# One TensorE loop body for both layers of a two-layer decode step

## The chip, the cores and the metric

One core of one Trainium2 chip runs the kernel as a single program. The metric is the device time of that program in microseconds. The core has five engines with instruction streams of their own: TensorE (PE in the profile; its weight loads are listed apart as PEld), VectorE (DVE), ScalarE (ACT), GpSimd (POOL) and SyncE (SP). Sixteen DMA engines move data between the device memory and the on-chip SBUF; TensorE adds up its products in eight PSUM banks of 128 partitions by 512 floats.

## The reference

The reference is one decode step of two equal layers. Each is a grouped-query attention over a cache of 32768 positions, followed by a gated feed-forward; both layers use the same caches and weights.

```
def layer(x):                                   # x: 2 x 1 x 512
    q = layernorm(x) @ wq                       # 2 x 32 heads x 128
    s = einsum("bhqd,bhkd->bhqk", q, k) * 128 ** -0.5   # 8 KV heads, 4 query heads on each
    o = einsum("bhqk,bhkd->bhqd", softmax(s), v)
    x = x + o.reshape(2, 1, 4096) @ wo
    g, u = layernorm(x) @ w_gate, layernorm(x) @ w_up   # 512 x 1792 each
    return x + (gelu(g) * u) @ w_down
out = layer(layer(x))
```

All is float32. The caches hold 2 x 8 x 32768 x 128 numbers each, and every layer needs all of both.

## The kernel before, in words

**Data.** SBUF has one pool, `mem`, of 110 units of 128 x 512 floats (256 KB each). The work of a layer is 16 pairs of a KV head and a batch row. A pair has 64 units of K and 64 of V, read in halves of 32 units, 8 MB each, and a half is 64 KB on each partition. The list `stream` holds all transfers in the order in which SP issues them; `plan` gives each its place in `mem`, and `pump` issues the next one as soon as its place is free. A place comes free when TensorE has multiplied with what lies there: SP waits for TensorE's semaphore and then issues. Layer 1 takes the pairs in the opposite order, so that K and V of the last pair of layer 0 serve the first pair of layer 1 without a second read. Because room is short there, six units are parked in the PSUM banks `S`, `T`, `M` during the change of layers (`stash`) and come back in the first pair's scores (line 728).

**A pair on TensorE.** `scores` (line 716) issues 64 products of 32 x 512, 32 into each bank of `S`. `softmax` follows on DVE and ACT with two small TensorE steps (lines 746, 759). `values` (line 782) issues 64 groups of two products of 16 x 512 into bank `A`, 128 in all, and `combine` (line 801) transposes four pieces. In layer 0 these go into `A`; in layer 1 they go into a bank of `M`. Line 811 (`project`) multiplies the first seven heads with `wo` in the last turn of a layer.

**The order of the work.** A recording layer (`Program`) notes every operation, derives the semaphore waits, and writes each engine's stream. ACT, DVE, POOL and SP get theirs straight. TensorE's is written by `run_tensor`: straight code (part 0), a loop over the 16 turns of layer 0, straight code (part 1), a loop over the 16 turns of layer 1, straight code (part 2). A loop body is values of turn n-1, then scores and softmax of turn n. Turn 0 of each layer (its scores and softmax) stands in the straight code ahead of the loop. A wait whose value differs from turn to turn reads a register, set before the loop and raised in each turn. What happens in one turn alone stands in the body under a branch (`apart`, `alone`, `more`).

**Between the layers.** After the last pair come the last head's product, `residual`, the gate and up products, `gelu`, the down product in pieces (`WD_SPLIT`), `residual` again, and the queries of layer 1, all fed by transfers of 0.25 to 2 MB. `warm` issues products that nobody reads.

**Banks there.** Layer 1's queries go into `A`, and so do layer 0's second `residual` and the first half of the scores of layer 1's turn 0:

```
        banks = [A, S[1]] if second else S
```

because `S[0]` holds a parked unit at that time.

Of the kernel before, what the change touches and what calls it, by code (L numbers as in the profile page):

```python
# [42 lines left out]
ROLLED = range(1, LAST + 1)  # L43
# [15 lines left out]
WO_PARTS = [[(0, 28), (28, 4)], [(4, 28), (0, 4)]]  # L59
# [62 lines left out]
class Program:  # L122
# [157 lines left out]
    def rolled(self, layer):  # L280


        by_place, apart, alone, more, waits = {}, {}, {}, {}, {}
        for op in self.ops:
            if op.turn and op.turn[0] == layer:
                if op.apart:
                    apart.setdefault(op.place, {}).setdefault(op.turn[1], []).append(op)
                else:
                    by_place.setdefault(op.place, []).append(op)
        order = sorted({*apart, *by_place}, key=lambda x: (SECTIONS.index(x[0]), x[1]))  # L290
        for place, ops in by_place.items():
            turns = [op.turn[1] for op in ops]
            assert turns == list(range(ROLLED[0], LAST + (place[0] == "values")))
            assert len({(o.where, str(o.extents), o.by) for o in ops}) == 1, "turns differ"
            waits[place] = here = []
            for key in {k for o in ops for k in o.waits}:
                v = [o.waits.get(key) for o in ops]
                known = [i for i, x in enumerate(v) if x is not None]
                if known == [len(ops) - 1] and turns[-1] == LAST:
                    low = max([x.value for x in self.ops[:ops[0].order] if x.key == key and x.by] or [0])  # L300
                    assert 0 < low < v[-1]
                    more.setdefault(turns[-2], []).append((place, key, v[-1] - low))
                    here.append((key, low, 0))
                    continue
                if len(known) < 3:
                    for i in known:
                        alone.setdefault(place, {}).setdefault(turns[i], []).append((key, v[i]))
                    continue
                steps = [(v[j] - v[i]) // (j - i) for i, j in zip(known, known[1:])]
                step = max(set(steps), key=steps.count)  # L310
                for i, o in enumerate(ops):
                    if v[i] is None:
                        near = min(known, key=lambda j: abs(i - j))
                        so_far = max([x.value for x in self.ops[:o.order] if x.key == key and x.by] or [0])
                        v[i] = min(max(v[near] + step * (i - near), 1), so_far)
                    assert v[i] > 0
                if v[1] < v[0] + step:
                    alone.setdefault(place, {}).setdefault(turns[0], []).append((key, v[0]))
                    v[0] = v[1] - step
                for i, (x, y) in enumerate(zip(v, v[1:])):  # L320
                    if y != x + step:
                        more.setdefault(turns[i], []).append((place, key, y - x - step))
                here.append((key, v[0], step))
        return order, by_place, waits, alone, more, apart

    def emit(self):
# [21 lines left out]
        def loop(e, layer):  # L348
            order, by_place, waits, alone, more, apart = self.rolled(layer)
            regs = {}  # L350
            for place, here in waits.items():
                for key, first, _ in here:
                    regs[place, key] = e.alloc_register(f"w{layer}_{len(regs)}")
                    e.reg_mov(regs[place, key], first)

            def places(section, n):
                for place in order:
                    if place[0] != section:
                        continue
                    for t in sorted({*alone.get(place, ()), *apart.get(place, ())}):  # L360
                        with e.If(n == t):
                            straight(e, apart.get(place, {}).get(t, ()))
                            for key, value in alone.get(place, {}).get(t, ()):
                                e.wait_ge(self.sems[key], value)
                    if place in by_place:
                        one(e, by_place[place][0], [(key, regs[place, key]) for key, _, _ in waits[place]])

            with e.Fori(ROLLED[0], LAST + 1) as n:
                places("values", n)
                with e.If(n != LAST):  # L370
                    places("project", n)
                    places("scores", n)
                    for t, here in sorted(more.items()):
                        with e.If(n == t):
                            for place, key, x in here:
                                e.reg_add(regs[place, key], regs[place, key], x)
                    for place, here in waits.items():
                        for key, _, step in here:
                            if step:
                                e.reg_add(regs[place, key], regs[place, key], step)  # L380

        def run_tensor(e):
# [39 lines left out]
SECTIONS = ["values", "project", "scores"]  # L422
# [11 lines left out]
def block_kernel(nc, x, kt, vt, wq, wo, gu, wd, out):  # L434
# [80 lines left out]
    def rolled(kind, l, n):  # L515
        return n in ROLLED if kind == "k" else True

    def add_wo(l, i):
        s, m = WO_PARTS[l][i]
        add(("wo", l, i), wo[:, s * DM:(s + m) * DM], m * DM)  # L520
# [94 lines left out]

    def heads(g):
# [53 lines left out]
    def queries(l):  # L670
        qp = small(A)
        for j, (s, m) in enumerate(pieces(WQ_SPLIT[l])):
            w = get(("wq", l, j), m)
            for i in range(s, s + m):
                (k, v), t = divmod(i // 4, 2), i % 4
                pe.matmul(qp[32 * t:32 * t + 32, :], window(k, v), w[:, i - s, :],  # L676
# [12 lines left out]
        for v in range(2):  # L689
            dve.tensor_copy(qin[:, :, v], src[:, :, :, NB * v:NB * v + NB].rearrange("p h t b -> p t b h"))  # L690
        return qt

    def stage(l, n):
        if n < len(ORDER):
            g, b = ORDERS[l][n]
            dve.tensor_copy(qpad, qall[:, REP * (NB * g + b):REP * (NB * g + b) + REP])

    def scores(l, n, g, b):
        first, second = meets(l, n)
        mx = tiny("mx")  # L700
        banks = [A, S[1]] if second else S
# [6 lines left out]
        for key, o, s, m in todo:  # L708
            if key is None:
                w = mem[:, o * UNIT:(o + m) * UNIT].rearrange("p (a c) -> p a c", a=m)  # L710
            else:
                w = get(key, at[key][0][1] if key in at else m)[:, o:o + m, :]
            for j in range(s, s + m):
                u, c, t = j // 32, j // QUAD % 8, j % QUAD
                tile_of = [i for i in order if i // 32 == u and i % QUAD == t]
                pe.matmul(banks[u][32 * t:32 * t + 32, :], pad[:, PAD_Q - 4 * c:PAD_Q + 32 - 4 * c],  # L716
                          w[:, j - s, :], start=(j == tile_of[0]), stop=(j == tile_of[-1]))
                if j == [i for i in order if i // 32 == u][-1]:
                    dve.tensor_reduce(mx[:, u:u + 1], banks[u], axis=AX.X, op=OP.max)  # L719
# [6 lines left out]
            elif second and key[1] == 0 and A_AT + o == BACK:  # L726
                for bank, i, copy in zip(where, range(WAIT), 3 * [act.copy, dve.tensor_copy]):
# [4 lines left out]
        return mx, banks  # L732
# [9 lines left out]
    def softmax(mx, banks):  # L742
# [9 lines left out]
        for u in range(2):  # L752
            act.activation(T[u], banks[u], AF.Exp, bias=bias, scale=SCALE, accum_out=ls[:, u:u + 1])  # L753
# [13 lines left out]
    def values(l, n, g, b, p):  # L767
# [23 lines left out]
    def combine(l, n, linv, g, b):  # L791
        if n == LAST - 1:
            act.activation(desk[:, :256], A[:, :256], AF.Copy, scale=linv)
            dve.tensor_scalar(desk[:, 256:], A[:, 256:], linv, None, op0=OP.mult)
            with pr.apart_of():
                warm(128, W[:NB], False)
        else:
            act.activation(desk, A, AF.Copy, scale=linv)  # L798
        m = small() if l else A
# [3 lines left out]
        dve.tensor_reduce(heads(g)[:, :, b], diag, axis=AX.XY, op=OP.add)  # L803

    def project(l):
        s, m = WO_PARTS[l][0]
        w = get(("wo", l, 0), m)
        turns = [g for g, _ in ORDERS[l][1::2]][:-1]
        for g in turns:
            for t in range(REP):  # L810
                pe.matmul(W[32 * t:32 * t + NB, :], heads(g)[:, t, :], w[:, REP * g + t - s, :],  # L811
                          start=(g == turns[0]), stop=(g == turns[-1]))
# [18 lines left out]
    def last_head(l, g):  # L831
        s, m = WO_PARTS[l][1]
        w = get(("wo", l, 1), m)
        for t in range(REP):
            add_row(heads(g)[:, t, :], w[:, t, :], t == REP - 1)
        done(("wo", l, 1))

    def residual():
# [5 lines left out]
        warm(128)  # L844
        m = small(A)[:, :2 * KC * NB].rearrange("p (i c b) -> p i c b", i=2, b=NB)
# [9 lines left out]
    def feedforward(l):  # L855
# [35 lines left out]
        tops = sum(WD_SPLIT[l][:1 if l else 2])  # L891
# [27 lines left out]
        for j, m in enumerate(WD_SPLIT[l]):  # L919
# [3 lines left out]
            elif not l and 1 <= j <= 2:  # L923
                if j == 1:
                    warm(256)
                    hidden(1)
                else:
                    warm(512)
# [14 lines left out]
    for l in range(2):  # L943
# [4 lines left out]
        for n in range(LAST + 1):  # L948
            with pr.turn_of(l, n) if n in ROLLED else nullcontext():
# [5 lines left out]
                if n == LAST - 1:  # L955
                    pr.section("project")
                    with pr.apart_of():
                        project(l)
                        turn(xin, side())
                pr.section("scores")  # L960
# [5 lines left out]
                found = softmax(*found)  # L966
# [4 lines left out]
        last_head(l, g)  # L971
        residual()
# [54 lines left out]
```

## Time and profile before

| what | value |
|---|---|
| median of 3 runs | 2557.25 us (2557.09 to 2557.37) |
| the profiled execution: its own time | 2557.27 us |
| its span, first to last instruction | 2555.8 us |
| TensorE busy, products | 1228.2 us, 48% of the span |
| read from device memory | 1102.58 MB, 431 GB/s over the span |
| mean granted TensorE clock | 0.748 |

The span leaves 1.47 us of the execution's time outside it. A busy share is a mean over the whole span; the rows below say which wait ends last in each stretch. Clock shares are of 2.4 GHz.

### The profile page before, as it was taken

Reading aid. Unit: us, or ns where it says so; the run is one execution under the profiler, and the core shown is the slowest. Engines: PE = TensorE matmul, PEld = TensorE weight load, DVE = VectorE, ACT = ScalarE, POOL = GpSimd, SP = SyncE. Lnnn points to the kernel's source line nnn. Section 1 sums busy time; section 2 is a strip of 40 time slices with the busy share of each in tenths; the row PEclk is TensorE's granted clock in tenths of the full one; section 3 lists DMA queues with packets and bytes.
Section 4 is the critical chain, followed back from the end, with each engine's and each line's share of the span. In section 5 each row is a group of like instructions: output and inputs, shape, how many; then the busy total and the mean of one; then the engine's idle time right before and its main releaser. Section 6 shows DMA issues by size and latency. Waiting matters only on the chain.

```text
span 2555.8 us, 19801 instructions
## 1 busy us (share of the span) xinstructions
PE 1228.2 (48%) x9177; PEld 320.9 (13%) x9177; DVE 145.8 (6%) x495; ACT 81.4 (3%) x189; POOL 2.7 (0%) x9
## 2 busy tenths in 40 slices
PE   3444445354455354354684553544544544534456
PEld 1011111011011011111121110111111111101112
DVE  0000000000000000000010000000000000000001
ACT  0000000000000000000000000000000000000000
POOL 0000000000000000000000000000000000000000
PEclk8677777777777777776897767777777777767788
DMA  9999999999999999999999999999999999999999
GB/s 426 428 439 431 435 432 431 438 432 437 431 431 436 432 437 431 435 432 431 427 418 436 434 433 436 433 433 434 431 437 432 435 433 432 435 433 434 434 433 386
DMA packets 25091, 1102.91 MB, mean 432 GB/s; under 512 B 2792, under 2 KB 2928, under 8 KB 5616
## 3 DMA queue, kind: packets, MB, share of 16 engines
q1 hardware_dynamic: 25056, 1102.65, 99.9%
q8 instruction: 12, 0.20, 0.0%
q14 instruction: 7, 0.06, 0.0%
q10 hardware_dynamic: 16, 0.00, 0.0%
HBM read 1102.58 MB, written 0.07 MB: 431 GB/s over the span
## 4 chain that ended last, share of the span: by engine, by line
DMA 74%; PE 23%; SPq 1%; another core or an unknown queue 0%; DVE 0%; issue 0%; ACT 0%
DMA mem<-in_kt 37%; DMA mem<-in_vt 35%; PE S L716 12%; PE A L782 11%; DMA mem<-in_wd 1%; SPq L487 1%; DMA mem<-in_wq 1%; DMA mem<-in_gu 1%; PE A L676 0%; PE W L829 0%; PE A L716 0%; ACT T L753 0%; DVE desk L755 0%; DVE aux L719 0%
## 5 line engine op out<-in xcount | busy, mean ns | idle before, releaser
L716 PE MATMUL S<-mem,aux 128*32 128x512 f32 x4032 | 512.1, 666 | 617.3 <-DMA mem<-in_kt 617.3
L782 PE MATMUL A<-mem 128*16 128x512 f32 x2048 | 292.3, 732 | 477.6 <-DMA mem<-in_vt 477.6
L782 PE MATMUL A<-mem,desk 128*16 128x512 f32 x2048 | 286.2, 722 | 32.4 <-DMA mem<-in_vt 17.7
L716 PEld LDWEIGHTS S<-mem,aux 128*32 128x32 f32 x4032 | 133.7, 121 | 972.6 <-DMA mem<-in_kt 639.7
L782 PEld LDWEIGHTS A<-mem 128*16 128x16 f32 x2048 | 62.2, 113 | 705.5 <-DMA mem<-in_vt 507.6
L719 DVE TENSOR_REDUCE aux<-S 128x1 f32<-128x512 f32 x63 | 43.5, 691 | 1130.7 <-PE S L716 1130.7
L782 PEld LDWEIGHTS A<-mem,desk 128*16 128x16 f32 x2048 | 64.6, 111 | 227.4 <-issue 209.4
L753 ACT ACTIVATE T<-S,aux 128x512 f32<-128x512 f32 x63 | 41.4, 657 | 1196.7 <-DVE aux L749 1196.7
L759 PE MATMUL M<-aux 128*128 128x4 f32 x64 | 14.5, 298 | 85.2 <-DVE aux L757 85.2
L798 ACT ACTIVATE desk<-A,aux 128x512 f32<-128x512 f32 x30 | 20.6, 687 | 1072.2 <-PE A L782 1072.2
L803 DVE TENSOR_REDUCE aux<-A 128x4 f32<-128x64 f32 x16 | 3.6, 226 | 551.8 <-PE A L801 551.8
L803 DVE TENSOR_REDUCE aux<-M 128x4 f32<-128x64 f32 x16 | 3.6, 226 | 512.6 <-PE M L801 512.6
L746 PE MATMUL M<-aux 128*128 128x128 f32 x32 | 10.3, 323 | 34.5 <-DVE aux L744 34.5
L755 DVE STREAM_TRANSPOSE desk<-T 128x512 f32<-128x512 f32 x32 | 22.9, 716 | 27.0 <-ACT T L753 27.0
L759 PEld LDWEIGHTS M<-aux 128*128 128x128 f32 x64 | 11.7, 229 | 91.3 <-DVE aux L757 91.3
L755 DVE STREAM_TRANSPOSE mem<-T 128x512 f32<-128x512 f32 x32 | 22.9, 717 | 0.0
L811 PE MATMUL W<-mem,aux 128*2 128x512 f32 x112 | 16.8, 765 | 12.4 <-DMA mem<-in_wo 12.4
L641 PE MATMUL W<-aux 128*128 128x256 f32 (+3 forms) x58 | 18.0, 392 | 1.0 <-DVE W L876 0.7
L676 PE MATMUL M<-mem,aux 128*32 128x512 f32 x64 | 9.5, 669 | 18.0 <-DMA mem<-in_wq 18.0
L801 PE MATMUL A<-aux,desk 128*128 128x128 f32 x64 | 10.1, 280 | 14.6 <-ACT desk L798 13.7
L801 PE MATMUL M<-aux,desk 128*128 128x128 f32 x64 | 10.7, 287 | 12.8 <-ACT desk L798 12.3
L753 ACT ACTIVATION_READ_ACCUMULATOR T<-S,aux 128x1 f32 x63 | 12.4, 196 | 0.0
(136 smaller groups left out, 191.5 us busy)
## 6 DMA issues: line engine op xcount, KB each, us to landing
mem<-in_wo SPq DMA_DIRECT2D x2, 7168.0 KB
mem<-in_vt SPq DMA_DIRECT2D x3, 4096.0 KB, 20.0
mem<-in_vt SPq DMA_DIRECT2D x1, 6144.0 KB, 29.2
mem<-in_gu SPq DMA_DIRECT2D x6, 896.0 KB, 28.2
mem<-in_gu SPq DMA_DIRECT2D x3, 1792.0 KB, 40.2
mem<-in_kt SPq DMA_DIRECT2D x1, 4864.0 KB, 17.6
mem<-in_vt SPq DMA_DIRECT2D x2, 2048.0 KB, 32.4
mem<-in_wd SPq DMA_DIRECT2D x4, 1024.0 KB, 21.6
```

Source lines behind the costliest of these rows:

```text
L487: sp.dma_start(at[key][1], src, sem=(key[0], key[4]) if plain else "any")
L641: pe.matmul(bank, ident[:, :bank.shape[0]], part.to_broadcast([P, n]), start=alone, stop=alone)
L716: pe.matmul(banks[u][32 * t:32 * t + 32, :], pad[:, PAD_Q - 4 * c:PAD_Q + 32 - 4 * c], w[:, j - s, :], start=(j == tile_of[0]), stop=(j == ...
L719: dve.tensor_reduce(mx[:, u:u + 1], banks[u], axis=AX.X, op=OP.max)
L746: pe.transpose(m[:, :P], nm.to_broadcast([P, P]), ident)
L753: act.activation(T[u], banks[u], AF.Exp, bias=bias, scale=SCALE, accum_out=ls[:, u:u + 1])
L755: dve.transpose(p[u], T[u])
L759: pe.matmul(m[:, :REP], both.to_broadcast([P, P]), same, start=True, stop=True)
L782: pe.matmul(A[32 * t:32 * t + 16, :], p[u][:, at_p:at_p + 16], w[:, QUAD * i + t, :], start=(j == order[0]), stop=(j == order[-1]))
L798: act.activation(desk, A, AF.Copy, scale=linv)
L801: pe.transpose(m[:, c * P:(c + 1) * P], desk[:, c * P:(c + 1) * P], ident)
L811: pe.matmul(W[32 * t:32 * t + NB, :], heads(g)[:, t, :], w[:, REP * g + t - s, :], start=(g == turns[0]), stop=(g == turns[-1]))
```

## The change

TensorE's stream now has one loop over the layers (twice) around one loop over 17 turns (n = 0 to 16): values unless n = 0, then scores and softmax unless n = 16. Turn 0 of both layers is in the body. The straight code between the layers stands in the outer loop under a branch and is followed by a jump back to the body. Ahead of the outer loop 160 waits on a semaphore that has long been reached (`ALIGN`) shift where the body lies. To make the turns of both layers equal, layer 1's heads are written to mirrored slots (`slot`), a second copy of `wo` with the heads in opposite order (`wr`) is an input, layer 1's queries and layer 0's second `residual` use `S[0]`, the unit parked there is copied to `A` by ACT in the feed-forward, layer 1's `combine` transposes into `A`, and three `warm` groups of layer 1's last pair are gone. In layer 0 three of the four pieces of the down product go in as wide products; before it was two.

```diff
-WO_PARTS = [[(0, 28), (28, 4)], [(4, 28), (0, 4)]]
+WO_PARTS = [(0, 28), (28, 4)]
...
         def run_tensor(e):
-            for part in range(3):
-                straight(e, [op for op in self.ops if op.eng == "PE" and not op.turn and op.part == part])
-                if part < 2:
-                    loop(e, part)
+            order, by_place, waits, alone, more, apart = self.rolled()
+            once = [[op for op in self.ops if op.eng == "PE" and not op.turn and op.part == i] for i in range(3)]
...
+            def enter(layer):
+                for place, here in waits.items():
+                    for key, first, _ in here:
+                        e.reg_mov(regs[place, key], first[layer])
...
+            straight(e, once[0])
+            for _ in range(ALIGN):
+                e.wait_ge(self.sems["ACT"], 1)
+            enter(0)
+            e.reg_mov(count, 0)
+            with e.Fori(0, 2) as l:
+                with e.Fori(0, LAST + 1) as n:
+                    with e.If(n != 0):
+                        section("values")
+                    with e.If(n != LAST):
+                        with e.If(n == LAST - 1):
+                            section("project")
+                        section("first")
+                        with e.If_ne(count, number_of((1, 0))):
+                            section("second")
+                        section("special", "softmax")
...
+                with e.If(l == 0):
+                    straight(e, once[1])
+                    enter(1)
+                    e.reg_add(count, count, 1)
+            straight(e, once[2])
...
+    def slot(l, g):
+        return HKV - 1 - g if l else g
...
     def queries(l):
-        qp = small(A)
+        qp = small(S[0])
...
     def scores(l, n, g, b):
-        banks = [A, S[1]] if second else S
...
-            if s and n == LAST - 1:
+            if s and n == LAST - 1 and not l:
                 with pr.apart_of():
                     warm(384, W[:NB], False)
...
-        m = small() if l else A
+        m = A
...
-        tops = sum(WD_SPLIT[l][:1 if l else 2])
+        tops = sum(WD_SPLIT[l][:1 if l else 3])
...
+            elif not l and j == 1:
+                warm(256)
+                hidden(1)
+                act.copy(A, S[0])
+            elif not l and j:
+                warm(512, S[0])
+                if j == 3:
                     turn(xin, side())
...
-            residual()
+            residual(S[0])
```

On TensorE, the end of the code between the layers and the start of layer 1 (`M`, `W`, `A`, `S` are PSUM banks, `mem` the pool, `aux` and `desk` small SBUF tiles) read before:

```order
L676 MATMUL A<-mem,aux 32x512 x4
L641 MATMUL W<-aux 128x256
L687 MATMUL W<-aux,desk 128x128 x4
L716 MATMUL A<-mem,aux 32x512 x32
L716 MATMUL S<-mem,aux 32x512 x32
L746 MATMUL M<-aux 128x128
L759 MATMUL M<-aux 128x4
L368 UNCONDITIONAL_BRANCH
L782 MATMUL A<-mem,desk 16x512 x16
```

and in the changed kernel:

```order
L708 MATMUL S<-mem,aux 32x512 x4
L672 MATMUL W<-aux 128x256
L719 MATMUL W<-aux,desk 128x128 x4
L413 REGISTER_ALU
L410 UNCONDITIONAL_BRANCH
L390 REGISTER_ALU
L390 COMPARE_AND_BRANCH
```

The scores of layer 1's turn 0 (line 716) no longer follow the queries' transposes (line 687, now 719) in the stream: the stream branches back to the loop body, which now holds them. The register settings of `enter(1)` stand between the transposes and that branch.

On TensorE, the down product of layer 0 up to the second `residual`, before (line 886 is a wide product, 829 a narrow one, 641 `warm`):

```order
L886 MATMUL W<-mem,aux 2x512 x4
L641 MATMUL A<-aux 128x512
L821 MATMUL W<-aux 2x128 x4
L824 MATMUL W<-desk,aux 2x128 x4
L829 MATMUL W<-mem,aux 2x128 x28
L641 MATMUL A<-aux 128x128
L846 MATMUL A<-aux,desk 128x16
```

and in the changed kernel:

```order
L921 MATMUL W<-mem,aux 2x512 x4
L672 MATMUL S<-aux 128x512
L921 MATMUL W<-mem,aux 2x512 x3
L672 MATMUL S<-aux 128x512
L857 MATMUL W<-aux 2x128 x4
L860 MATMUL W<-desk,aux 2x128 x4
L865 MATMUL W<-mem,aux 2x128 x16
L672 MATMUL S<-aux 128x128
L881 MATMUL S<-aux,desk 128x16
```

Three units moved from narrow products (12 of the 28) to three wide ones, and the turn of `x` (lines 857, 860) moved behind them. On ACT, the same place, from the last step of `gelu` to the first unit that comes back, before:

```order
L866 ACTIVATE desk<-desk,aux 128x256
L819 ACTIVATE desk<-W 128x512
L843 ACTIVATE desk,aux<-W 128x128
L684 ACTIVATE desk<-A,aux 128x256 x2
L728 COPY mem<-S 128x512
```

and in the changed kernel:

```order
L901 ACTIVATE desk<-desk,aux 128x256
L961 COPY A<-S 128x512
L855 ACTIVATE desk<-W 128x512
L878 ACTIVATE desk,aux<-W 128x128
L716 ACTIVATE desk<-S,aux 128x256 x2
L764 COPY mem<-A 128x512
```

One row is added: line 961, the copy of the parked unit, stands ahead of the step that reads `W` for the turn (line 855), and line 764, which brings the unit back, now reads `A`. SP's list of transfers is the same in sizes and order; two of them read `wr` in place of `wo`.

## Rows read from the trace of the kernel before

**Rows 1.** The page, first part: busy us, share of the span, instructions.
```profile
PE 1228.2 (48%) x9177; PEld 320.9 (13%) x9177; DVE 145.8 (6%) x495; ACT 81.4 (3%) x189; POOL 2.7 (0%) x9
```
**Rows 2.** The page, DMA queues: packets, MB, share of 16 engines.
```profile
q1 hardware_dynamic: 25056, 1102.65, 99.9%
q8 instruction: 12, 0.20, 0.0%
q14 instruction: 7, 0.06, 0.0%
```
**Rows 3.** Chain of waits in order of time, layer 1: start us, us, what.
```profile
1403.71 9.47 PE S L716 x64
1413.20 29.18 DMA mem<-in_vt
1442.42 8.88 PE A L782 x64
1451.32 29.77 DMA mem<-in_kt
```
**Rows 4.** The page, DMA issues: count and median us from issue to landing.
```profile
mem<-in_kt SPq DMA_DIRECT2D x61, 39.5
mem<-in_vt SPq DMA_DIRECT2D x59, 31.0
out<-desk SPq DMA_DIRECT2D x1, 64.0 KB, 1.5
```
**Rows 5.** Stretches: us, busy us of engines (instructions), PEclk, DMA share, GB/s.
```profile
150.00:1240.00 1090.00, 508.69 (x3754) 129.17 (x3754) 55.35 (x182) 30.47 (x71) 0.00 (x0) 0.73 1.00 434
2495.00:2522.00 27.00, 11.29 (x69) 2.84 (x69) 2.97 (x10) 1.45 (x4) 0.00 (x0) 0.73 0.97 418
2549.00:2550.00 1.00, 0.42 (x6) 0.26 (x10) 0.42 (x1) 0.48 (x1) 0.00 (x0) 1.00 0.84 336
2550.00:2551.00 1.00, 1.00 (x41) 0.87 (x40) 0.17 (x1) 0.00 (x0) 0.00 (x0) 1.00 0.57 213
2551.00:2552.00 1.00, 0.58 (x24) 0.38 (x20) 0.00 (x0) 0.00 (x0) 0.00 (x0) 1.00 0.22 86
2552.00:2553.00 1.00, 0.89 (x36) 0.58 (x28) 0.00 (x0) 0.00 (x0) 0.00 (x0) 1.00 0.05 20
```
**Rows 6.** Chain of waits, the end.
```profile
2522.53 30.23 DMA mem<-in_wd
2552.80 0.62 PE W L829 x16
2553.45 0.45 PE W L829 x8
2553.91 0.29 DVE desk L977
```
**Rows 7.** DMA queues of the stretch 0 to 150 us.
```profile
q8 instruction: 4, 0.07, 0.2%
```
**Rows 8.** DMA queues of 150 to 1280 us, all rows.
```profile
q1 hardware_dynamic: 8964, 489.49, 100.1%
q14 instruction: 3, 0.02, 0.0%
```
**Rows 9.** DMA queues of 1280 to 1380 us.
```profile
q8 instruction: 6, 0.10, 0.4%
```
**Rows 10.** DMA queues of 2530 to 2556 us.
```profile
q8 instruction: 2, 0.03, 0.5%
```
**Rows 11.** DMA issues of 1302 to 1332 us: size, us from issue to landing.
```profile
mem<-in_wq SPq DMA_DIRECT2D x4, 1024.0 KB, 7.5
```
**Rows 12.** Chain of waits, start of layer 1.
```profile
1330.37 0.75 PE W L687 x4
1331.14 0.20 DVE aux L690
1331.60 0.18 DVE aux L696
1331.83 2.83 PE A L716 x24
1350.78 0.58 PE M L759 x2
1351.36 0.58 issue
```
**Rows 13.** TensorE at the start: start, us, line [idle before <- releaser].
```profile
34.55 0.80 PE L687 MATMUL M<-aux,desk 128*128 128x128 f32 x4 [1.93 <-ACT desk L684]
42.06 1.94 PE L716 MATMUL S<-mem,aux 128*32 128x512 f32 x8 [6.71 <-DMA mem<-in_kt]
```
**Rows 14.** The page, costliest groups: busy, mean ns of one | idle before.
```profile
L803 DVE TENSOR_REDUCE aux<-M 128x4 f32<-128x64 f32 x16 | 3.6, 226 | 512.6 <-PE M L801 512.6
```

**Rows 15.** Chain of waits, the start.
```profile
0.74 0.38 SPq L487
1.18 40.75 DMA mem<-in_kt
```

More of the change, by code (lines that the diff above doesn't have):

```diff
@@ L42 @@
 LAST = 16
-ROLLED = range(1, LAST + 1)
+ALIGN = 160
 A_AT, B_AT, C_AT, ROOM_AT = 0, CHUNK, 2 * CHUNK, 3 * CHUNK
@@ L278, in number, with rolled @@
                 op.waits[x.key] = max(op.waits.get(x.key, 0), x.value)
-    def rolled(self, layer):
+    def rolled(self):
         by_place, apart, alone, more, waits = {}, {}, {}, {}, {}
         for op in self.ops:
[L285 to L289, printed above, removed]
+            if op.turn and op.apart:
+                apart.setdefault(op.place, {}).setdefault(op.turn, []).append(op)
+            elif op.turn:
+                by_place.setdefault(op.place, {})[op.turn] = op
@@ L290, in rolled @@
         order = sorted({*apart, *by_place}, key=lambda x: (SECTIONS.index(x[0]), x[1]))
         for place, ops in by_place.items():
-            turns = [op.turn[1] for op in ops]
-            assert turns == list(range(ROLLED[0], LAST + (place[0] == "values")))
-            assert len({(o.where, str(o.extents), o.by) for o in ops}) == 1, "turns differ"
+            assert len({(o.where, str(o.extents), o.by) for o in ops.values()}) == 1, "turns differ"
             waits[place] = here = []
[L296 to L303, printed above, removed]
-                    continue
[L305 to L323, printed above, removed]
@@ new lines, in rolled, with so_far @@
+            layers = [sorted(t for t in ops if t[0] == layer) for layer in range(2)]
+            for key in {k for o in ops.values() for k in o.waits}:
+                def so_far(t):
+                    return max([x.value for x in self.ops[:ops[t].order] if x.key == key and x.by] or [0])
+                known = [[t for t in layer if key in ops[t].waits] for layer in layers]
+                few = max(map(len, known)) < 3 and max(map(len, layers)) > 2
+                late = all(t[1] == LAST for some in known for t in some) and all(so_far(x[0]) for x in layers)
+                if few and not late:
+                    for some in known:
+                        for t in some:
+                            alone.setdefault(place, {}).setdefault(t, []).append((key, ops[t].waits[key]))
+                    continue
+                want = {t: ops[t].waits[key] for some in known for t in some}
+                steps = [] if few else [(want[u] - want[t]) // (u[1] - t[1])
+                                        for some in known for t, u in zip(some, some[1:])]
+                step = max(set(steps), key=steps.count) if steps else 0
+                first = []
+                for layer, some in zip(layers, known):
+                    for t in layer:
+                        if t in want:
+                            continue
+                        near = min(some, key=lambda u: abs(u[1] - t[1])) if some and not few else None
+                        limit = so_far(layer[0] if near is None else t)
+                        want[t] = min(max(want[near] + step * (t[1] - near[1]), 1), limit) if near else limit
+                    if len(layer) > 1 and want[layer[1]] < want[layer[0]] + step:
+                        if layer[0] in some:
+                            alone.setdefault(place, {}).setdefault(layer[0], []).append((key, want[layer[0]]))
+                        want[layer[0]] = want[layer[1]] - step
+                    assert all(want[t] > 0 for t in layer)
+                    l, n = layer[0]
+                    now = max(want[layer[0]] - step * n, 0)
+                    first.append(now)
+                    for i in range(LAST):
+                        now += step
+                        if (l, i + 1) in want and now != want[l, i + 1]:
+                            more.setdefault((l, i), []).append((place, key, want[l, i + 1] - now))
+                            now = want[l, i + 1]
+                here.append((key, first, step))
@@ L346, in run, with run_tensor, number_of, section @@
             straight(e, [op for op in self.ops if op.eng == eng])
[L348 to L356, printed above, removed]
+        def run_tensor(e):
+            order, by_place, waits, alone, more, apart = self.rolled()
+            once = [[op for op in self.ops if op.eng == "PE" and not op.turn and op.part == i] for i in range(3)]
+            regs = {(place, key): e.alloc_register(f"w{i}")
+                    for i, (place, key) in enumerate((p, k) for p in waits for k, _, _ in waits[p])}
+            count = e.alloc_register("count")
+            def number_of(t):
+                return (LAST + 1) * t[0] + t[1]
+            def enter(layer):
+                for place, here in waits.items():
+                    for key, first, _ in here:
+                        e.reg_mov(regs[place, key], first[layer])
+            def section(*names):
                 for place in order:
-                    if place[0] != section:
+                    if place[0] not in names:
                         continue
                     for t in sorted({*alone.get(place, ()), *apart.get(place, ())}):
-                        with e.If(n == t):
+                        with e.If_eq(count, number_of(t)):
                             straight(e, apart.get(place, {}).get(t, ()))
@@ L365, in places @@
                     if place in by_place:
[L366 to L380, printed above, removed]
@@ L382, in run_tensor @@
-        def run_tensor(e):
-            for part in range(3):
-                straight(e, [op for op in self.ops if op.eng == "PE" and not op.turn and op.part == part])
-                if part < 2:
-                    loop(e, part)
+                        op = next(iter(by_place[place].values()))
+                        one(e, op, [(key, regs[place, key]) for key, _, _ in waits[place]])
+            straight(e, once[0])
+            for _ in range(ALIGN):
+                e.wait_ge(self.sems["ACT"], 1)
@@ new lines, in run_tensor @@
+            enter(0)
[11 more added lines that the diff above has]
+                        section("special", "softmax")
+                        for t, here in sorted(more.items()):
+                            with e.If_eq(count, number_of(t)):
+                                for place, key, x in here:
+                                    e.reg_add(regs[place, key], regs[place, key], x)
+                        for place, here in waits.items():
+                            for key, _, step in here:
+                                if step:
+                                    e.reg_add(regs[place, key], regs[place, key], step)
+                        e.reg_add(count, count, 1)
+                with e.If(l == 0):
+                    straight(e, once[1])
+                    enter(1)
+                    e.reg_add(count, count, 1)
@@ L419, in __getattr__ @@
         return call
-SECTIONS = ["values", "project", "scores"]
+SECTIONS = ["values", "project", "first", "second", "special", "softmax"]
 C_ID = 0
@@ L726, in scores @@
             elif second and key[1] == 0 and A_AT + o == BACK:
-                for bank, i, copy in zip(where, range(WAIT), 3 * [act.copy, dve.tensor_copy]):
+                for bank, i, copy in zip([A, *where[1:]], range(WAIT), 3 * [act.copy, dve.tensor_copy]):
                     copy(mem[:, (BACK + i) * UNIT:(BACK + i + 1) * UNIT], bank)
@@ L956, in block_kernel @@
                     pr.section("project")
[L957 to L960, printed above, removed]
+                    project(l)
+                    turn(xin, side())
                 state["next"] = 0
```

83 lines of the change are left out of this document (42 added, 41 removed).

## The prediction

> **What bounds the kernel now.** I read the page's busy shares first: TensorE, the busiest engine, is at 48% [rows 1]. Then the DMA queues: the data queue q1 fills 99.9% of 16 engines' time with 1102.65 MB [rows 2]. A kernel whose transfers leave no gap can only be made faster by moving fewer bytes, moving them faster, or shortening the two ends where no transfer runs. The chain of waits seems to say otherwise, since TensorE's scores and values stand in it between transfers [rows 3]: 9.47 us of scores, 29.18 us of V, 8.88 us of values, 29.77 us of K. But that chain goes from a freed place to the transfer that uses it; another transfer runs meanwhile. The DMA issues show it: a K half is 8.39 MB, which at the 434 GB/s of the steady stretch [rows 5] takes 19.3 us, yet it lands 39.5 us after its issue, and a V half 31.0 us after [rows 4]. So a K half waits 20.2 us and a V half 11.7 us (medians) behind transfers that are still running. TensorE may be late by that much in every pair and nothing moves. I take 11.7 us as the cover of the loop. The bytes are the same in the changed kernel, in the same order and sizes, so that 0.2% (5.1 us, about what a measurement of this kernel can tell from no change) would have to come from the ends, from queue q8, or from a wait that eats its cover.
>
> **What is left at the end.** In the four microseconds from 2549 to 2553 the DMA share falls as 0.84, 0.57, 0.22, 0.05 [rows 5]: the 16 engines do not finish together. The last piece of the down weights that the chain shows lands at 2552.76 [rows 6]. The unused share up to there is 0.16 + 0.43 + 0.78 + (0.76 - 0.05) = 2.1 us: were all engines equally late, the data would be in 2.1 us sooner. One thing that makes engines unequal is instruction traffic: q8 carried 12 packets with 0.20 MB, q14 7 with 0.06 MB [rows 2]. The q8 packets come with new TensorE code: 4 in the first 150 us, when the stream gets into its first loop, none in the turns after that, where only q14 has packets [rows 8], 6 between 1280 and 1380 us, 2 after 2530 [rows 7, 9, 10]; 4 + 6 + 2 = 12 leaves none for the later turns of the second loop either. A packet is 0.20 MB / 12 = 16.7 KB, and one engine of 16 moves 434 / 16 = 27 GB/s, so a packet costs one engine at least 0.6 us; I call up to 1.2 us possible, since the place it writes to may be slower (an estimate). As the queue never runs dry, an engine that lost 0.6 us stays that late to the end.
>
> **The change part by part.**
>
> *Fewer code packets.* The changed stream is shorter by one loop body and one set of turn-0 scores, and layer 1's body is not new code when it comes. The 6 packets of the change of layers and the 2 of the end are what can go; the 4 of the start stay. All that these 8 can be worth is bounded by the 2.1 us of unequal finish on one side and by nothing on the other, if the latest engine is late for another reason (q14, the start). They are 8 of 19 packets but 0.13 of 0.26 MB, half of it: I take half of 2.1, that is -1.0 us, ends -2.1 and 0.
>
> *The 160 waits ahead of the loop and the register settings.* No row prices one such wait. The nearest is the entry of layer 1's loop, where 12 register settings stand between line 759 and the first values: from the start of the former at 1350.78 to the end of the "issue" at 1351.94 are 1.16 us [rows 12], so 0.1 us each at most. 160 of them take 0 to 16 us, and if two go together 8. TensorE is idle there for 6.71 us [rows 13], and what is over (at most 9.3 us) delays the release of the first K half, whose successor is issued with the cover of a K half, 20.2 us. Cost 0; without that cover it would be 9.3 us once.
>
> *Branches in each turn.* The body has about a dozen more branches and settings than before: 12 x 0.1 = 1.2 us a turn against 11.7 us of cover. In layer 1 the four transposes now go into `A`, which the next values cannot overwrite until DVE's reduction has read it: 0.226 us and a handover [rows 14]. Together under 2 us a turn: cost 0, and 32 x 2 = 64 us if there were no cover at all.
>
> *Between the layers* the cover is thinnest. A 1 MB piece lands 7.5 us after its issue [rows 11]; at 418 GB/s (the stretch from 2495 us, the nearest row to small pieces) [rows 5] it takes 2.5 us, so 5.0 us lie between issue and start. Of these up to 1.5 us are the way of any transfer, as the output's 64 KB show [rows 4]. 3.5 us remain. The queries' transposes start at 1330.37; before, the scores start at 1331.83, after two DVE copies [rows 12]. Now 13 register settings and some 8 branches come after the transposes are handed over: 2.1 us, beside 1331.83 - 1330.37 - 0.75 = 0.7 us of DVE that was waited for anyway. So scores start up to 1.4 us later, which releases the next K pieces 1.4 us later, inside 3.5. ACT's copy of a bank stands between a DVE copy and `warm`, and the three wide products that replace 12 narrow ones shorten the way after the last down piece. Cost 0 for all, ends 0 and +1.4 us (if the cover is gone).
>
> *The end.* The three `warm` groups of layer 1's last pair are gone. The granted clock is 0.73 in 2495 to 2522 us and 1.00 after 2549 [rows 5]. Should it stay at the lower level (1.2 GHz), the last eight products after the last landing take up to 0.45 us more [rows 6]. The other `warm` groups stay, so 0, ends 0 and +0.45.
>
> **Sum**: 2557.27 us (the profiled execution; the median of the runs, 2557.25, is the same) - 1.0 + 0 = 2556.3 us.
>
> **The rivals.**
>
> *Nothing is gained (2557.2 us).* The latest engine is late for other reasons, or the packets that go are replaced by others at the same places. For it: only some engines had code packets, and the end waits for one engine. Against: half of the instruction bytes.
>
> *The jump back starves the transfers (2560 us).* TensorE jumps from the end of the code between the layers back to the loop body. If that code is no longer in the store, it comes by q8 while TensorE waits, at the one place where the cover is 3.5 us. Such a packet has to wait for data packets too: two or three in turn, each with a K packet of 64 KB ahead of it (64 KB at 27 GB/s is 2.4 us, and 0.6 us for its own) are 6 to 9 us of delay; over 3.5 us the transfers stand still for the rest, 2.5 to 5.5 us, so 2559 to 2562. Against: after the first turns the loop branches of before brought no packet [rows 8].
> The Trainium skill (Runtime: NRT & Kernel Launch, Instruction fetch mechanics) says that prefetch is sequential and that a taken branch to code outside the current window of pages forces a fetch before execution goes on. It speaks for this rival. The trace agrees in part: code came with each straight stretch, but the taken branches of later turns brought none.
>
> *The body does not fit (2562 us or more; the other side).* If body and branches are longer than the store keeps, each turn fetches again. The price: 4 packets a turn, as many as the first loop took, over 32 turns are 128 packets of 0.6 to 1.2 us, shared by 16 engines 4.8 to 9.6 us. It decides as soon as q8 shows packets in the steady stretches. Against: a turn of before needs none, and the new body adds only the branches and the second half of one turn's scores.
>
> *More than 5.1 us faster.* All time without full transfers is the 1.2 us up to the first issues [rows 15] and the way of the first data, the unequal finish of 2.1, and the 2.4 us from the last products [rows 6] to the end of the span; nothing here touches the first and third. Only a higher transfer rate would do it.
>
> **How the numbers follow.** Forecast (0.4 to 2.1 us gained) 0.57; nothing gained (within 0.4 us) 0.25; starved jump 0.08; body that does not fit 0.06; faster by over 0.2% 0.03; the rest, 0.01, is a cost nobody named. Of the starved jump 0.07 lies within 5.1 us of before and 0.01 beyond. So faster 0.03, slower 0.06 + 0.01 + 0.01 = 0.08 at most, of which I take 0.07 since a body that barely does not fit ends within the bound; same 0.90. The range starts at 2554.8, a little under the -2.1 us end (2555.2), and goes up to 2559.6, which takes in the ends of +1.4 and +0.45 and the lower part of the starved jump.
>
> **What would show it.** Right: q8 with 4 to 7 packets, none in the turns of either layer and none or few after 2530 us; the DMA share at 1.00 in both steady stretches and in the change of layers; a shorter slope at the end. The entry of the values and the transposes in layer 1 may be later without any effect. Wrong: q8 with dozens of packets, a DMA share under 0.97 at 1330 to 1345 us, or a gap of TensorE at the first scores of layer 1 that is longer than the K pieces' cover. The forecast fails as a whole if the steady rate is not 434 GB/s, since a tenth of a percent of it is 2.5 us.

## The result, and the profile after

| what | before | after |
|---|---|---|
| median of 6 runs | 2557.42 us (2557.09 to 2557.95) | 2567.59 us (2566.54 to 2568.70) |
| ratio | | 1.0039, 95% interval 1.0026 to 1.0052 |
| span of the profiled execution | 2555.8 us | 2565.7 us |

The change makes the kernel 10.2 us (0.39%) slower. The forecast was 2556.3 us, the range ended at 2559.6: it was wrong.

The page's DMA queues after (packets, MB, share of 16 engines), which answer to [rows 2]:

```profile
q1 hardware_dynamic: 25056, 1102.65, 99.6%
q8 instruction: 8, 0.13, 0.0%
```

The data queue moved the same packets in a longer span. Busy times by stretch (columns as in [rows 5]) show where it stood still:

```profile
150.00:1240.00 1090.00, 506.50 (x3754) 134.75 (x3754) 55.44 (x182) 30.48 (x71) 0.00 (x0) 0.73 1.00 433
1430.00:2496.00 1066.00, 501.62 (x3679) 132.50 (x3671) 52.40 (x171) 29.04 (x67) 0.00 (x0) 0.73 1.00 434
1336.00:1338.00 2.00, 2.00 (x16) 0.67 (x12) 0.00 (x0) 0.00 (x0) 0.00 (x0) 0.53 0.59 201
1384.00:1385.00 1.00, 0.00 (x0) 0.00 (x0) 0.00 (x0) 0.00 (x0) 0.00 (x0) 0.50 0.01 0
1385.00:1391.00 6.00, 5.34 (x32) 1.04 (x32) 0.00 (x0) 0.00 (x1) 0.00 (x0) 0.66 0.00 0
```

Both layers' turns run at the rate of before (DMA share 1.00, 433 and 434 GB/s; layer 0 moved 0.66 MB less in its stretch than before, but had moved 0.52 MB more by 150 us). The time is lost between them: 7 us with a share of 0.00 or 0.01 from 1384 to 1391, and 41% of 2 us at 1336. With what follows (a share of 1.55 in 1391 to 1393, when the queue starts again, and of 0.08 in 1393 to 1395) the stop costs 11 - 3.1 - 0.2 = 7.7 us of data queue. These 8.5 us are most of the 9.9 us by which the span grew. Another 0.7 us is there before them: the last piece of `wq` lands at 1328.73 us, before at 1328.01. The rest is not placed. The chain of waits (start us, us, what) says who was late. After:

```profile
1333.08 1.24 issue
1334.32 15.70 PE S L752 x126
1355.61 8.45 PE A L819 x64
1364.08 21.46 DMA mem<-in_vt
1385.58 5.39 PE A L819 x32
1390.99 21.86 DMA mem<-in_kt
```

and the same place before:

```profile
1351.94 16.61 PE A L782 x128
1368.56 35.11 DMA mem<-in_kt
```

Before, layer 1's first values are one block of 128 matmuls (16.61 us), since their V lies in SBUF from layer 0. (The trace has two matmuls for each product of the code: these 128 are the 64 products that `values` issues, which the description of the kernel before counts as 128.) After, they stop after 96, wait for a V transfer that was issued at 1364.08, in the middle of these very values, and go on at 1385.58. TensorE's timeline (start, us, engine line, out<-in, [idle before <- releaser]):

```profile
1385.58 5.34 PE L819 MATMUL A<-mem 128*16 128x512 f32 x32 [18.14 <-DMA mem<-in_vt]
```

18.14 us of idle time, for a transfer that these products do not read. So the next K, which goes where that V lies, is issued at 1390.99 and not at 1368.56: 22.4 us late. It used to land 35.11 us after its issue; now it lands after 21.86, since the data queue is empty when it is issued. The difference, 13.2 us, is the time that it used to wait behind other transfers: its cover.

**Where the wait comes from.** A wait that only a layer's last turn needs stands in the loop body with its value in a register, and so it now stands in the turns of both layers. Layer 0's last turn reads its last pieces of V (units 48 and 56) under semaphores that many transfers share. Layer 1 has no such need at unit 48, but the register must hold something:

```
limit = so_far(layer[0] if near is None else t)
```

`so_far` is the newest value that the semaphore will have had when the recorded program comes to this place. At unit 48 the register starts with 16 and 160 for the two layers; 160 is the value left by the second 16-unit V piece of the next pair. That is free of deadlock, since the transfer is issued ahead of it, and harmless in layer 0, where 16 was reached long ago. In layer 1's first values the newest transfer is one that has just been issued.

### The profile page after: what moved, and what is told of

The parts are those of the page before. It is cut to its first block, busy times and chain, and to the rows that moved or that the text cites. A ratio compares the mean times of both kernels' runs of the same rounds, so it can differ in the third digit from the quotient of the medians.

```text
span 2565.7 us, 20148 instructions
## 1 busy us (share of the span) xinstructions
PE 1232.3 (48%) x9155; PEld 334.0 (13%) x9155; DVE 146.0 (6%) x495; ACT 82.2 (3%) x190; POOL 2.7 (0%) x9
## 4 chain that ended last, share of the span: by engine, by line
DMA 74%; PE 24%; SPq 1%; issue 1%; DVE 0%; ACT 0%; ACTq 0%
DMA mem<-in_vt 36%; DMA mem<-in_kt 35%; PE S L752 12%; PE A L819 11%; DMA mem<-in_wd 1%; SPq L515 1%; DMA mem<-in_wq 1%; DMA mem<-in_gu 0%; PE S L708 0%; PE A L936 0%; PE W L865 0%; PE S L672 0%; PE W L921 0%; PE W L672 0%; ACT T L790 0%
## 5 line engine op out<-in xcount | busy, mean ns | idle before, releaser
L752 PE MATMUL S<-mem,aux 128*32 128x512 f32 x4096 | 519.6, 665 | 605.1 <-DMA mem<-in_kt 581.4
L752 PEld LDWEIGHTS S<-mem,aux 128*32 128x32 f32 x4096 | 150.7, 121 | 952.3 <-DMA mem<-in_kt 608.6
L839 PE MATMUL A<-aux,desk 128*128 128x128 f32 x128 | 20.9, 286 | 26.8 <-ACT desk L836 24.6
L839 PEld LDWEIGHTS A<-aux,desk 128*128 128x128 f32 x128 | 13.4, 140 | 55.6 <-ACT desk L836 52.2
```

The costliest lines, as they stand in the source:

```text
L752: pe.matmul(S[u][32 * t:32 * t + 32, :], pad[:, PAD_Q - 4 * c:PAD_Q + 32 - 4 * c], w[:, j - s, :], start=(j == tile_of[0]), stop=(j == til ...
L839: pe.transpose(m[:, c * P:(c + 1) * P], desk[:, c * P:(c + 1) * P], ident)
```

## The experiments

**e1.** The changed kernel, where layer 1 starts from the value that layer 0's last turn has waited for (48 in place of 160 at unit 48, and 32 in place of 128 at unit 56).

```diff
                         limit = so_far(layer[0] if near is None else t)
+                        if few and layer is layers[1] and known[0]:
+                            limit = max(ops[u].waits[key] for u in known[0])
```

> Edit: in the changed kernel the two registers (the waits before the eighth-size V pieces) start layer 1 with the value that layer 0's last turn has already waited for, in place of the newest value recorded. Theory W (a made-up wait): in the changed kernel TensorE stops 18.1 us in layer 1's first values for a V piece that belongs to the next pair; K is issued 22.4 us later than before and the data queue stands still for 7.5 us at 1384 to 1392 us. Without it: the stop gone, values of that turn in one piece of about 17 us, data queue without a gap there, time 2567.6 - 8 = 2559.5 us (2558.5 to 2560.5). Rival J (jump back, branches and the single bank A make layer 1's turns late): no change, 2567 to 2568 us, and the stop stays.

Measured: 2558.99 us (11 runs), before in the same job 2557.26; ratio 1.0006 (0.9997 to 1.0015). 8.6 us of the 10.2 are gone. The chain has one block of values again and K goes out at 1371.25:

```profile
1355.94 15.29 PE A L821 x128
1371.25 35.01 DMA mem<-in_kt
```

Theory W holds. J is out as the cause of the 8.6 us: the jump, the branches and the single bank are all still there.

**e2.** The kernel before with that wait added to layer 1's first values at unit 48.

```diff
+        if layer == 1:
+            later = next(op for op in self.ops if op.turn == (1, 2) and op.place == ("values", 16))
+            (key, value), = [(k, v) for k, v in later.waits.items() if k[0] in ("any", "v")]
+            alone.setdefault(("values", 48), {}).setdefault(1, []).append((key, value))
```

> Edit: the kernel before, with one more wait in layer 1's first values, ahead of the pieces that start at unit 48: for the second 16-unit V piece of the next pair. Theory W: the stop of about 18 us and the gap of about 7.5 us in the data queue appear, time 2557.4 + 8 = 2565.5 us (2564 to 2566.5). Rival J: that wait is covered like all others, 2557.4 us.

Measured: 2565.89 us (5 runs), 8.6 us above before; ratio 1.0035 (1.0022 to 1.0048). Chain, then stretches:

```profile
1361.75 22.01 DMA mem<-in_vt
1384.01 5.65 PE A L786 x32
1389.68 22.91 DMA mem<-in_kt
```
```profile
1381.00:1384.00 3.00, 0.00 (x0) 0.00 (x0) 0.00 (x0) 0.00 (x0) 0.00 (x0) 0.50 0.23 98
1384.00:1390.00 6.00, 5.59 (x32) 1.03 (x32) 0.00 (x0) 0.32 (x1) 0.00 (x0) 0.66 0.01 3
```

One wait in the old program makes the same stop and the same gap: 3 x 0.77 + 6 x 0.99 = 8.3 us of data queue, near the 8.6 us of time. e1 takes the wait out and e2 puts it in, and both move the time by 8.6 us: that this wait costs it is shown.

**e4.** The same, but for the first 16-unit piece (`("values", 0)` in the edit's first line).

> Edit: the kernel before, with one more wait at the same place as in e2_before_with_wait, but for the first 16-unit V piece of the next pair, which lands about 9.5 us earlier. Theory W with a cover: TensorE stops for about 8 us, K is issued some 12 to 13 us later than before, inside the cover of 22.4 - 7.5 = 15 us; no gap in the data queue, 2557.4 us as before. Rival (every stop of TensorE there costs its length): 2557.4 + 8 = 2565 us.

Measured: 2557.34 us (10 runs); ratio 1.0002 (0.9992 to 1.0011).

```profile
1358.07 16.71 DMA mem<-in_vt
1375.03 6.11 PE A L786 x32
1381.16 23.89 DMA mem<-in_kt
```
```profile
1368.00:1380.00 12.00, 4.97 (x24) 0.98 (x28) 0.00 (x0) 0.00 (x0) 0.00 (x0) 0.57 1.01 433
1380.00:1392.00 12.00, 8.75 (x80) 2.52 (x72) 0.92 (x2) 0.69 (x1) 0.00 (x0) 1.00 1.01 416
```

K is issued 1381.16 - 1368.56 = 12.6 us late and the data queue does not notice. With e2 (21.1 us late, 8.3 lost: a cover of 12.8) this agrees with the 13.2 us read above. Of the two waits, the one within the cover cost nothing and the one beyond it cost what was over.

**e3.** What e1 leaves is 1.7 us by the medians, within the interval (-0.8 to +3.8 us); but 9 of e1's 11 runs are over 2558.3 us and none of the 28 of before. It was sought in the register settings: e1 with `enter(1)` ahead of `straight(e, once[1])`.

> Edit: as e1_passed_value, and the 13 register settings for layer 1 stand ahead of the code between the layers in place of behind it. Theory W with thin cover: the settings cost 13 x 0.0875 = 1.1 us on the way to layer 1's first scores, and the 0.9 us short gap of the data queue at 1336 us comes from there; with them moved scores start 0.7 to 1.1 us earlier, the gap at 1336 us goes, time 0.4 to 0.9 us below e1_passed_value, about 2558.8 us. Rival: the branches alone (1.2 us) keep the gap, no difference from e1_passed_value.

Measured: 2559.97 us (11 runs, 2556.93 to 2560.94); ratio 1.0009 (1.0000 to 1.0018). A miss: it is no better. The gap at 1336 us did go, but two others came where the settings now stand (chain, then stretches):

```profile
1283.09 1.16 issue
```
```profile
1286.00:1287.00 1.00, 1.00 (x6) 0.92 (x5) 0.00 (x0) 0.37 (x2) 0.00 (x0) 0.50 0.45 185
1290.00:1291.00 1.00, 1.00 (x7) 0.40 (x9) 0.17 (x2) 0.00 (x0) 0.41 (x1) 0.50 0.66 164
```

The clock column reads 0.50 there (1.2 GHz), as it does in the gap of after at 1336 (0.53 above). TensorE is idle for the 1.16 us in which its sequencer sets registers, and what follows runs at the lower level. The stretch at 1336 us in the kernel before, then two rows of e1:

```profile
1336.00:1338.00 2.00, 2.00 (x24) 0.65 (x20) 1.52 (x3) 1.06 (x3) 0.00 (x0) 1.00 1.01 422
```
```profile
1336.00:1338.00 2.00, 2.00 (x13) 0.59 (x9) 0.00 (x0) 0.00 (x0) 0.00 (x0) 0.50 0.51 135
1338.00:1340.00 2.00, 2.00 (x24) 0.86 (x20) 0.00 (x0) 0.00 (x0) 0.00 (x0) 0.96 0.89 356
```

e1 has 13 matmuls in 2 us where before has 24, and 24 itself in the next 2 us: the K pieces are released late because TensorE is slow, not only because it starts late.

**e6.** e1 with one setting ahead of each of the last 13 waits for a transfer between the layers.

```diff
                 with e.If(l == 0):
-                    straight(e, once[1])
-                    enter(1)
+                    todo = [(regs[place, key], first[1]) for place, here in waits.items() for key, first, _ in here]
+                    spots = [op for op in once[1] if any(isinstance(key, tuple) for key in op.waits)][-len(todo):]
...
+                    for op in once[1]:
+                        if op in spots:
+                            e.reg_mov(*todo.pop(0))
+                        straight(e, [op])
```

> Edit: as e1_passed_value, and the 13 register settings for layer 1 stand one each ahead of the last 13 waits for a transfer in the code between the layers. Theory C (what is left in e1_passed_value, 1.7 us, comes from TensorE's 2.5 us of idle time before layer 1's first scores, after which the granted clock reads 0.50 for 3.4 us): the idle time falls to about 1.4 us, the clock stays at 1.00 over 1332 to 1346 us as in the kernel before, no gap of the data queue at 1336 us, 2557.3 to 2558.3 us. Rival K (the 1.7 us come from the 16 DMA engines' unequal finish): the gap goes but the time stays at 2559.0 us.

Measured: 2557.43 us (11 runs; before 2557.21); ratio 1.0001 (0.9992 to 1.0010). TensorE's timeline, then the stretch:

```profile
1332.30 4.93 PE L759 MATMUL S<-mem,aux 128*32 128x512 f32 x44 [1.38 <-DVE W L990]
```
```profile
1336.00:1338.00 2.00, 2.00 (x24) 0.76 (x20) 1.90 (x3) 1.53 (x3) 0.00 (x0) 1.00 1.12 451
```

1.38 us of idle time, clock 1.00, no gap, and 10 of 11 runs at 2557.74 us or less. This is what theory C expected, and not what rival K did. But the scores also start earlier here (1332.30 us, in e1 1334.65), so e6 alone does not tell the clock from the late start.

**e8.** e1 with one unread product behind the transposes of layer 1's queries.

```diff
             pe.transpose(qt[:, h * P:(h + 1) * P], desk[:, h * P:(h + 1) * P], ident)
+        if l:
+            warm(512, S[0])
```

> Edit: as e1_passed_value, and one more product that nobody reads (512 columns, into the free bank S[0]) behind the transposes of layer 1's queries, which TensorE works on while its sequencer does the settings and branches. Theory C: idle time before the first scores falls from 2.5 to about 1.4 us, the clock reads 1.00 over 1332 to 1346 us, the scores start no earlier (1334.7 us), K pieces are released 1 us or more earlier than in e1_passed_value, the gap at 1336 us shrinks from 1.2 us to 0.3 us or less, 2557.8 to 2558.6 us. Rival (the lower clock follows from something else): clock at 0.50 again, time as e1_passed_value, 2559.0 us.

Measured: 2557.70 us (11 runs); ratio 1.0003 (0.9994 to 1.0012).

```profile
1334.10 3.21 PE L756 MATMUL S<-mem,aux 128*32 128x512 f32 x28 [1.65 <-issue]
```
```profile
1336.00:1338.00 2.00, 2.00 (x26) 0.68 (x18) 0.19 (x1) 0.24 (x1) 0.00 (x0) 1.00 0.95 332
```

The scores start 3.3 us after the queries' transposes, as in e1 (1334.10 after 1330.79, and 1334.65 after 1331.35), but the clock stays at 1.00 and 5% of these 2 us are lost in place of 49%. By the medians 1.2 of the 1.7 us go with the lower clock, and 0.5 are left for the late start; both are within the intervals.

What holds the clock up is not shown as surely. Each kernel has one profile. In those of after, e1 and e7 (below) the clock also reads 0.50 or 0.51 in 1294 to 1297 us, in those of e6, e8 and e9 it reads 1.00, with the same products there and 1.4 us of idle time at 1291 us in all six. So the idle time alone does not decide, and e7 is no slower for it.

**e9.** e6 and e8 together.

> Edit: e6_spread_settings and e8_keep_busy together. Theory C: as e6_spread_settings or a little better, 2557.2 to 2558.2 us, and no slower than the kernel before by more than 0.5 us; the code packets (8 in place of 12) could bring it below the kernel before. Rival K: 2559.0 us.

Measured: 2557.26 us (11 runs; before 2557.21); ratio 1.0000 (0.9991 to 1.0009). Level with before, with 8 code packets in place of 12. The hoped-for gain is not there. The end:

```profile
2549.00:2550.00 1.00, 0.68 (x14) 0.51 (x18) 0.44 (x2) 0.22 (x1) 0.00 (x0) 1.00 0.98 385
2550.00:2551.00 1.00, 0.95 (x36) 0.63 (x25) 0.00 (x0) 0.00 (x0) 0.00 (x0) 1.00 0.54 193
2551.00:2552.00 1.00, 0.39 (x16) 0.41 (x20) 0.00 (x0) 0.00 (x0) 0.00 (x0) 1.00 0.07 29
2552.00:2553.00 1.00, 0.93 (x38) 0.62 (x32) 0.00 (x0) 0.00 (x0) 0.00 (x0) 1.00 0.05 20
```

Most engines seem to be nearer together than in [rows 5] (0.98 and 0.54, then 0.07), but the last is as late: the last piece of the down weights lands at 2552.69 us, before at 2552.76.

**e7.** e6 without the 160 waits.

```diff
-ALIGN = 160
+ALIGN = 0
```

> Edit: as e6_spread_settings with ALIGN = 0, that is without the 160 waits ahead of the loop. Theory S (the waits place the body so that body and what follows stay in the store): without them queue q8 carries more than 8 packets, some in the turns; each costs one DMA engine about 1 us, so up to 2 us slower than e6_spread_settings if a handful come on top and 5 us or more if every turn fetches. Rival: 8 to 12 packets as in both kernels, time within 0.7 us of e6_spread_settings.

Measured: 2557.41 us (10 runs); ratio 1.0002 (0.9992 to 1.0011); 8 code packets, none in the turns. Theory S is out for this program: the placement makes no difference that the runs can show.

No version beat the kernel before; e6 to e9 are level with it.

## Why the prediction was wrong

**What bounds the kernel: right.** Both steady stretches kept their rate, and the cover of transfers by transfers decides which of the delays cost time.

**The step that failed is "Branches in each turn", at cost 0.** It priced what the body adds by the time of branches and settings, 1.2 us, and never asked what the registers hold. The change adds waits to turns that had none; one of them is for the newest transfer. That step says "together under 2 us a turn"; one turn had 18.14. K was 22.4 us late. The data queue itself was 1.5 us late by then (0.7 ahead of 1328 us, 0.8 at 1336), the cover took 13.2, and the 7.7 us that are left are the stop of the queue; without the wait (e1) the time is 8.6 us less. The rule that fills a register without a known value stood in the changed kernel, in lines that the excerpt of the change leaves out, and the forecast named no wait that the change adds. It even said that the entry of the values in layer 1 may be later without any effect.

**Between the layers: right about the late scores, wrong about the price.** It gave up to 1.4 us of lateness for the first scores and a cost of 0, at most +1.4 us. They start 1334.32 - 1331.83 = 2.5 us later. 0.7 us of it is older, since the transposes start 0.7 us later too (1331.01, before 1330.31); the other 1.8 are settings and branches. The settings came every 0.0875 us, but in the trace's records of TensorE's sequencer four of the five compare-and-branches ahead of the scores take 0.26 us each up to the next instruction, not 0.1. All this lies within the cover of 3.5 us, which should have held. What the forecast left out is the granted clock: after 2.50 us of idle time the stretch at 1336 us reads 0.53, and TensorE releases the K pieces more slowly too. Its own sign of being wrong came: a DMA share under 0.97 at 1330 to 1345 us (0.59 in 1336 to 1338). It marked the smaller loss. e1 less before is 1.7 us, and e6 takes 1.6 of it back.

**Fewer code packets: -1.0 us forecast, 0 measured** (e9 less before, 0.05 us). 8 packets came, not 4 to 7: 4 at the start, 2 between the layers, 2 at the end. The rival "nothing is gained" is what the runs show for this term: the last landing was not made earlier. The term took half of the 2.1 us of unequal finish in one profile. In e4, with 12 packets as before, the same sum (0.97, 0.96, 0.52 and 0.21 from 2549 us on, last landing at 2552.83) is 1.2 us, at the same time of 2557.3 us: the slope differs from one execution to the next and does not say what can be gained.

**The 160 waits and the end: the cost was right, the account of the delay in part luck.** The first scores start 7.6 us later than in [rows 13] (forecast up to 9.3):

```profile
49.66 1.93 PE L752 MATMUL S<-mem,aux 128*32 128x512 f32 x7 [13.73 <-issue]
```

It costs nothing: when the next V transfer is issued, at 71.97 us (before 71.82), the delay is all but gone. But without the 160 waits (e7) the scores start at 47.46 us, with them (e6) at 49.54: taking them out gives back 2.1 us. The trace's records of TensorE's sequencer show what else holds them up. The waits end at 44.29 us, 8.8 us after they begin, much as forecast. Then the branch by which turn 0 jumps over the values (line 392) takes 2.72 us, where its median over the 34 turns is 0.075; in e7 it takes 8.54 us. A code packet starts at 46 us (in e7 at 44), and one more at 53 us, in a second stop of 4.09 us (51.59 to 55.67). So TensorE most likely waits for code there. The forecast had this mechanism for the jump between the layers and not for the start. The clock at the end is 1.00 as before.

**The rivals.** "The jump back starves the transfers" had the right symptom, transfers that stand still at the change of layers, and the wrong cause. No code came at the jump, which comes after 1332 us; queue q8 between 1280 and 1400 us has two packets, both ahead of 1320 us:

```profile
q8 instruction: 2, 0.03, 0.1%
```

By the Trainium skill (Runtime: NRT & Kernel Launch, Instruction fetch mechanics) a taken branch to code outside the current window forces a fetch. The trace agrees at the start (the branch of 2.72 us, with its packet), but the jump back to layer 1's turns, over all the code between the layers, brought no packet, and none of the branches there took over 0.21 us. "The body does not fit" came nearest in time (2562 us or more) and was wrong too: no packet in any turn.

## What to carry to other kernels

When two programs are folded into one loop, list the waits that each turn gets and that it did not have, and for each the transfer that leaves its value: one that "has surely been issued" may be one that has just been issued. In a kernel bound by transfers, take the lead of each transfer (issue to landing, less its own time) as the budget: here a delay inside it (12.6 us of 13.2) was free, and what went beyond it was paid in full (e2). Register settings and branches in a row leave TensorE idle (2.50 us here), and part of the price can be in the clock that follows.

## What was not expected of the hardware

2.50 us without a product ahead of layer 1's scores were followed by a granted clock of 0.53 in 1336 to 1338 us; 1.65 and 1.38 us at the same place were not (1.00 in e8 and e6). Shorter idle times did precede a lower clock elsewhere: 1.16 us in e3, and 1.4 us at 1291 us in three of six profiles. What decides it, no run here separates. In after all DMA engines stand still from 1384 to 1391 us, and yet they finish unequally again (a share of 0.71, 0.13 and 0.06 in the microseconds from 2560 to 2563).
